# Converting double-precision weights on chip: from seven VectorE operations a chunk to two VectorE, four ScalarE and two GpSimd operations

## Chip, cores and metric

One core of a Trainium2 chip. The metric is the device time of one execution in microseconds, median of several runs. Ratios below are the mean time of one kernel's fast runs over the mean of the other's of the same rounds, so not quite the ratio of the medians. A difference counts as faster or slower from 2%. The rounds ran on different chips; the kernel before was run in each, with medians from 1779.24 to 1780.69 us, while the changed kernel has the four runs of its first measurement only.

## The reference

```python
# attention: q, k, v are (8, 8, 576, 64)
scores = matmul(q, k.T) / 8
scores = where(scores >= max(scores) - tau, scores, -1e9)
attn = softmax(scores);  x = attn @ v          # then (B, H, S, D) -> (B, S, 512)
# feed-forward, with weights that arrive as float64
xn = (x - mean) / sqrt(var + 1e-6) * g_ln
out = x + maximum(xn @ w_ch1, 0) @ w_ch2       # w_ch1 (512, 2048), w_ch2 (2048, 512)
```

## The kernel before

The work goes batch by batch, with no inner barrier: while the attention of batch b is computed, the feed-forward group b-1 is woven in. A batch has four head pairs of five "points"; a point is two sides (two heads), the fifth has one, so a batch has 36 sides. For every side: scores on TensorE, row maximum `neg` (VectorE), threshold `thr` (GpSimd), exponential `e` (ScalarE), mask and sum (VectorE), normalisation of `e` (GpSimd), transposes `tp` (TensorE), copy to `em` (ScalarE), value matmuls `pv`.

The weights come as 8-byte doubles, 32 chunks of 128x512, 16 for w1 (read during batch 0) and 16 for w2 (read from the end of batch 0 into batch 1). The kernel uses no double-precision arithmetic; a chunk's words are put together as float32 by bit operations:

```python
raw = pool.tile([128, WC], I64, tag="sq", name="raw")        # two buffers, shared with the feed-forward
nc.gpsimd.dma_start(out=raw, in_=src)
lo, hi = words[:, :, 0], words[:, :, 1]
nc.vector.tensor_scalar(out=p, in0=hi, ... shift right 20, and 0x7FF)       # L172
nc.vector.tensor_scalar(out=p, in0=p, ... add -896, max 0)                  # L176
nc.vector.tensor_scalar(out=p, in0=p, ... shift left 23)                    # L179
nc.vector.scalar_tensor_tensor(out=p, in0=hi, in1=p, ... sign)              # L182
nc.vector.tensor_scalar(out=a, in0=hi, ... shift left 3, and 0x7FFFF8)      # L186
nc.vector.tensor_tensor(out=a, in0=a, in1=p, op=ALU.bitwise_or)             # L190
nc.vector.scalar_tensor_tensor(out=b, in0=lo, scalar=2.0**-52, in1=p, ...)  # L191
nc.gpsimd.tensor_tensor(out=s, in0=a, in1=b, op=ALU.add)                    # L194
if gi is not None:
    nc.scalar.mul(dst, s, g_sb[:, gi : gi + 1])                             # L196, w1 alone
```

The program is scheduled by a framework that reorders instructions and then fixes the order on each engine. Each engine keeps that order, so an instruction that waits holds all behind it (below, a ScalarE copy that waits 4.86 us, with others behind it).

## Time and profile before

1780.69 us, median of 3 (1779.36 to 1781.99; with a fourth run 1780.68). The marks are read from the order of time on GpSimd: the start of the 1st, 25th and 37th threshold operation (`thr`), and of `sa`, the first sum of a feed-forward group.

| | before |
|---|---|
| thr 1 | 23.2 us |
| thr 25 (24 sides later) | 111.7 us |
| thr 37 (one batch after thr 1) | 158.7 us |
| first `sa` (batch 0 is done) | 171.8 us |
| second `sa` | 380.0 us, 208.2 later |
| end of the span | 1778.9 us, 1398.9 later |

The last line contains no conversion. What is won must be won before the second `sa`.

### The profile page before, as it was taken

What the parts mean: (1) busy time and instruction counts of PE and PEld (TensorE: products, weight loads), DVE (VectorE), ACT (ScalarE), POOL (GpSimd) and SP (SyncE); (2) the same over time, 40 slices, a digit from 0 to 9 for tenths busy, and PEclk for the clock granted to TensorE, in tenths of its full rate; (3) what the DMA queues carried; (4) which work ended last, traced back from release to release, by engine and by line L of the source; (5) the groups of instructions that cost most, each with busy time, mean ns of one, the idle gap of its engine ahead of it and who ended that gap; (6) DMA issues with size and microseconds to landing.
All of it is one profiled execution on the core that took longest, in us unless ns stands there. A gap on an engine that the chain in (4) does not pass through costs nothing.

```text
span 1778.9 us, 19810 instructions
## 1 busy us (share of the span) xinstructions
PE 1671.1 (94%) x6974; PEld 851.8 (48%) x6974; DVE 747.9 (42%) x1719; ACT 558.2 (31%) x1108; POOL 503.3 (28%) x756
## 2 busy tenths in 40 slices
PE   4887889999999999999999999999999999999998
PEld 2444344545555455545554555545544555444443
DVE  6888794443333433433344333443344334200000
ACT  2443233224322442234323432244223432220110
POOL 4555552241222222232224122222233122300100
PEclk8877999999999999999999999999999999999999
DMA  7232341111111110111111111111011000001001
GB/s 140 69 78 68 85 115 21 32 33 20 21 25 22 27 22 17 33 27 21 21 32 33 21 21 25 22 28 21 16 33 26 8 1 12 13 0 16 8 3 21
DMA packets 271379, 55.83 MB, mean 31 GB/s; under 512 B 267184, under 2 KB 267184, under 8 KB 271280
## 3 DMA queue, kind: packets, MB, share of 16 engines
q1 hardware_dynamic: 266640, 37.78, 12.6%
q0 software_dynamic: 4640, 16.78, 3.1%
q8 instruction: 55, 0.90, 0.2%
q14 instruction: 44, 0.36, 0.1%
HBM read 45.09 MB, written 9.44 MB: 31 GB/s over the span
## 4 chain that ended last, share of the span: by engine, by line
PE 80%; DVE 8%; ACT 4%; POOL 4%; DMA 2%; issue 1%; SPq 0%; POOLq 0%; DVEq 0%; ACTq 0%
PE p L394 27%; PE p L359 25%; PE pv L316 11%; PE sc L230 10%; PE tp L281 6%; DVE neg L239 3%; ACT e L247 2%; DMA raw<-in_moe_w_ch_dram 2%; ACT em L284 1%; DVE xc L342 1%; PE tr L290 1%; DVE e L254 1%; ACT er L297 1%; DVE p L182 1%; PE tr L292 1%
## 5 line engine op out<-in xcount | busy, mean ns | idle before, releaser
L359 PE MATMUL p<-xc,w 128*128 128x512 f32 x1152 | 542.0, 609 | 12.1 <-DVE xc L342 11.6
L394 PE MATMUL p<-h,w 128*128 128x512 f32 x1152 | 525.2, 597 | 0.0
L239 DVE TENSOR_REDUCE neg<-sc 128x1 f32<-128x576 f32 x288 | 207.5, 749 | 459.0 <-PE sc L230 459.0
L247 ACT ACTIVATE e<-sc,neg 128x576 f32<-128x576 f32 x288 | 212.8, 745 | 392.8 <-DVE neg L239 390.5
L359 PEld LDWEIGHTS p<-xc,w 128*128 128x128 f32 x1152 | 208.6, 194 | 227.8 <-issue 210.7
L394 PEld LDWEIGHTS p<-h,w 128*128 128x128 f32 x1152 | 206.6, 190 | 218.5 <-issue 218.0
L259 POOL TENSOR_SCALAR e<-e,den 128x576 f32<-128x576 f32 x288 | 216.5, 754 | 258.7 <-DVE den L258 229.5
L242 POOL TENSOR_SCALAR thr<-neg,low_sb 128x1 f32<-128x1 f32 x288 | 91.3, 317 | 627.4 <-DVE neg L239 604.6
L254 DVE SCALAR_TENSOR_TENSOR e<-sc,thr,e 128x576 f32<-128x576 f32 x288 | 232.0, 812 | 49.0 <-ACT e L247 32.6
L230 PE MATMUL sc<-kT,qT 64*128 64x288 f32 x1024 | 194.5, 453 | 29.7 <-DVE kT L208 16.5
L284 ACT COPY em<-tp 128x512 f32<-128x512 f32 x256 | 149.2, 583 | 205.1 <-PE tp L281 202.8
L364 ACT ACTIVATE h<-p 128x512 f32<-128x512 f32 x144 | 86.0, 597 | 383.0 <-PE p L359 382.8
L281 PEld LDWEIGHTS tp<-ident,e 128*128 128x128 f32 x1152 | 135.8, 145 | 135.7 <-ACT em L284 59.4
L281 PE MATMUL tp<-ident,e 128*128 128x128 f32 x1152 | 190.1, 290 | 8.0 <-ACT em L284 4.0
L316 PE MATMUL pv<-em,v_in 128*64 128x256 f32 (+1 forms) x1536 | 177.2, 351 | 19.3 <-ACT em L284 10.1
L230 PEld LDWEIGHTS sc<-kT,qT 64*128 64x128 f32 x1024 | 105.2, 196 | 139.3 <-issue 76.8
L316 PEld LDWEIGHTS pv<-em,v_in 128*64 128x64 f32 x1536 | 99.4, 143 | 124.0 <-ACT em L284 33.6
L402 POOL TENSOR_TENSOR o<-o,x 128x512 f32<-128x512 f32 x36 | 45.5, 1264 | 274.1 <-DVE o L401 274.1
L401 DVE TENSOR_TENSOR o<-p,rb 128x512 f32<-128x512 f32 x36 | 24.9, 691 | 200.8 <-PE p L394 200.8
L327 DVE COPY x<-pv 128x256 f32<-128x256 f32 (+3 forms) x120 | 35.3, 311 | 161.9 <-PE pv L316 161.9
L316 PE MATMUL pv<-er,v_rest 128*64 128x256 f32 (+1 forms) x384 | 64.8, 346 | 14.5 <-ACT er L299 14.5
L297 ACT COPY er<-tr 64x128 f32<-64x128 f32 x256 | 65.7, 257 | 1.7 <-PE tr L292 0.2
(59 smaller groups left out, 827.8 us busy)
## 6 DMA issues: line engine op xcount, KB each, us to landing
raw<-in_moe_w_ch_dram POOLq DMA_DIRECT2D x32, 512.0 KB, 4.3
q_in<-in_q_dram SPq DMA_DIRECT2D x128, 72.0 KB, 2.5
k_in<-in_k_dram SPq DMA_DIRECT2D x128, 72.0 KB, 2.3
out_dram<-ot SPq DMA_DIRECT2D x144, 64.0 KB, 2.0
v_in<-in_v_dram SPq DMA_DIRECT2D x64, 128.0 KB, 2.5
v_rest<-in_v_dram SPq DMA_DIRECT2D x64, 16.0 KB, 2.2
tau_sb<-in_tau_dram SPq DMA_DIRECT2D x1, 0.5 KB, 2.6
g_sb<-in_moe_g_ln_dram POOLq DMA_DIRECT2D x1, 2.0 KB, 3.3
```

What stands on the lines that cost most here:

```text
L230: nc.tensor.matmul(sc[:, c, :HALF], lhsT=lhsT, rhs=kT[rows, c * HALF : (c + 1) * HALF], start=True, stop=True,)
L239: nc.vector.tensor_reduce(out=neg[:, i : i + 1], in_=sc[:, :, :HALF], axis=AXL.XY, op=ALU.max, negate=True)
L242: nc.gpsimd.tensor_scalar(out=thr[:, i : i + 1], in0=neg[:, i : i + 1], scalar1=-1.0, scalar2=low_sb, op0=ALU.mult, op1=ALU.add,)
L247: nc.scalar.activation(e.rearrange("p (c n) -> p c n", c=2), sc[:, :, :HALF], func=AF.Exp, bias=neg[:, i : i + 1],)
L254: nc.vector.scalar_tensor_tensor(out=e2, in0=sc[:, :, :HALF], scalar=thr[:, i : i + 1], in1=e2, op0=ALU.is_ge, op1=ALU.mult, accum_out=den ...
L259: nc.gpsimd.tensor_scalar(out=e, in0=e, scalar1=den[:, i : i + 1], scalar2=1.0, op0=ALU.mult, op1=ALU.mult)
L281: nc.tensor.transpose(tp[:, c], e[:, c * 128 : (c + 1) * 128], ident)
L284: nc.scalar.copy(em[:, :, h, o : o + 128], tp)
L316: nc.tensor.matmul(pv[64 * h : 64 * h + 64, :n], lhsT=vt[:, c, h, :] if c < J else vr[:, h, :], rhs=em[:, c, h, :n] if c < J else er[:, :n ...
L359: nc.tensor.matmul(p1, lhsT=w1_sb[c][:, d * 128 : (d + 1) * 128], rhs=xc[:, c, :], start=(c == 0), stop=(c == NK - 1),)
L364: nc.scalar.activation(h, p1, func=AF.Relu)
L394: nc.tensor.matmul(p2, lhsT=w2_sb[d][:, m * 128 : (m + 1) * 128], rhs=hs[d], start=(d == 0), stop=(d == ND - 1),)
```

## The change

Intent: take the conversion off VectorE, which is busy six to nine tenths in each slice of the first 270 us. The high word is shifted as a whole (two VectorE operations), the low word is scaled to an integer by ScalarE and added as an integer by GpSimd, so that a carry runs into the exponent by itself. Three more ScalarE operations make a factor that is the gain for normal numbers and zero for tiny ones, and GpSimd multiplies by it.

```diff
-  (the seven VectorE operations, L194 on GpSimd and L196 on ScalarE)
+  a = pool.tile([128, WC], U32, tag="o", name="w_bits")
+  r = pool.tile([128, WC], I32, tag="rb", bufs=1, name="w_low")
+  m = pool.tile([128, WC], F32, tag="ot", name="w_kept")
+  nc.scalar.activation(r, lo, func=AF.Copy, scale=2.0**-29)                   # L185
+  nc.scalar.activation(m, <hi as f32>, func=AF.Square)                        # L186
+  nc.scalar.activation(m, m, func=AF.Sign, bias=tiny_sb)                      # L190
+  nc.scalar.activation(m, m, func=AF.Identity, scale=gh, bias=gh)             # L192
+  nc.vector.tensor_scalar(out=a, in0=hi, ... shift left 3, and 0x3FFFFFFF)    # L193
+  nc.vector.scalar_tensor_tensor(out=a, in0=hi, scalar=0xC0000000, in1=a, ...)# L197
+  nc.gpsimd.tensor_tensor(out=a, in0=a, in1=r, op=ALU.add)                    # L201, int32
+  nc.gpsimd.tensor_tensor(out=dst, in0=a, in1=m, op=ALU.mult)                 # L202
```

`gh` is half the gain (w1) or 0.5 (w2), made once on GpSimd.

More of the change, by code (lines that the diff above doesn't have):

```diff
@@ L10 @@
 U32 = mybir.dt.uint32
+I32 = mybir.dt.int32
 I64 = mybir.dt.int64
@@ L74 @@
     g_sb = consts.tile([128, NK], F32, name="g_sb")
+    g_half = consts.tile([128, NK], F32, name="g_half")
+    half_sb = consts.tile([128, 1], F32, name="half_sb")
+    tiny_sb = consts.tile([128, 1], F32, name="tiny_sb")
     ident = consts.tile([128, 128], F32, name="ident")
@@ L122 @@
     nc.vector.memset(avg_sb, 1.0 / DM)
+    nc.vector.memset(half_sb, 0.5)
+    nc.vector.memset(tiny_sb, -(1.0625 * 2.0**-15) ** 2)
     nc.vector.tensor_scalar(
@@ L136 @@
     nc.gpsimd.dma_start(out=g_sb, in_=g_ln.rearrange("(c p) -> p c", p=128))
+    nc.gpsimd.tensor_scalar(
+        out=g_half, in0=g_sb, scalar1=0.5, scalar2=1.0, op0=ALU.mult, op1=ALU.mult
+    )
     WC = 512
@@ L160, in weight_steps @@
         for dst, src, gi in chunks:
-            s = pool.tile([128, WC], F32, tag="o", name="w_sum") if gi is not None else dst
             if src.dtype != I64:
-                nc.gpsimd.dma_start(out=s, in_=src)
-            else:
-                raw = pool.tile([128, WC], I64, tag="sq", name="raw")
-                nc.gpsimd.dma_start(out=raw, in_=src)
-                words = raw.bitcast(U32).rearrange("p (n two) -> p n two", two=2)
-                lo, hi = words[:, :, 0], words[:, :, 1]
-                p = pool.tile([128, WC], U32, tag="o", name="p")
-                a = pool.tile([128, WC], U32, tag="ot", name="a")
-                b = pool.tile([128, WC], F32, tag="ot", name="b")
-                nc.vector.tensor_scalar(
-                    out=p, in0=hi, scalar1=20, scalar2=0x7FF,
-                    op0=ALU.logical_shift_right, op1=ALU.bitwise_and,
-                )
-                nc.vector.tensor_scalar(
-                    out=p, in0=p, scalar1=-896.0, scalar2=0.0, op0=ALU.add, op1=ALU.max
-                )
-                nc.vector.tensor_scalar(
-                    out=p, in0=p, scalar1=23, scalar2=None, op0=ALU.logical_shift_left
-                )
-                nc.vector.scalar_tensor_tensor(
-                    out=p, in0=hi, scalar=0x80000000, in1=p,
-                    op0=ALU.bitwise_and, op1=ALU.bitwise_or,
-                )
-                nc.vector.tensor_scalar(
-                    out=a, in0=hi, scalar1=3, scalar2=0x7FFFF8,
-                    op0=ALU.logical_shift_left, op1=ALU.bitwise_and,
-                )
-                nc.vector.tensor_tensor(out=a, in0=a, in1=p, op=ALU.bitwise_or)
-                nc.vector.scalar_tensor_tensor(
-                    out=b, in0=lo, scalar=2.0**-52, in1=p.bitcast(F32), op0=ALU.mult, op1=ALU.mult
-                )
-                nc.gpsimd.tensor_tensor(out=s, in0=a.bitcast(F32), in1=b, op=ALU.add)
@@ L195, in weight_steps @@
-            if gi is not None:
-                nc.scalar.mul(dst, s, g_sb[:, gi : gi + 1])
+                nc.gpsimd.dma_start(out=dst, in_=src)
+                if gi is not None:
+                    nc.scalar.mul(dst, dst, g_sb[:, gi : gi + 1])
+                yield
+                continue
+            raw = pool.tile([128, WC], I64, tag="sq", name="raw")
+            nc.gpsimd.dma_start(out=raw, in_=src)
+            words = raw.bitcast(U32).rearrange("p (n two) -> p n two", two=2)
+            lo, hi = words[:, :, 0], words[:, :, 1]
@@ new lines, in weight_steps @@
+            a = pool.tile([128, WC], U32, tag="o", name="w_bits")
+            r = pool.tile([128, WC], I32, tag="rb", bufs=1, name="w_low")
+            m = pool.tile([128, WC], F32, tag="ot", name="w_kept")
+            nc.scalar.activation(r, lo, func=AF.Copy, scale=2.0**-29)
+            nc.scalar.activation(
+                m, raw.bitcast(F32).rearrange("p (n two) -> p n two", two=2)[:, :, 1],
+                func=AF.Square,
+            )
+            nc.scalar.activation(m, m, func=AF.Sign, bias=tiny_sb)
@@ new lines, in weight_steps @@
+            gh = half_sb if gi is None else g_half[:, gi : gi + 1]
+            nc.scalar.activation(m, m, func=AF.Identity, scale=gh, bias=gh)
+            nc.vector.tensor_scalar(
+                out=a, in0=hi, scalar1=3, scalar2=0x3FFFFFFF,
+                op0=ALU.logical_shift_left, op1=ALU.bitwise_and,
+            )
+            nc.vector.scalar_tensor_tensor(
+                out=a, in0=hi, scalar=0xC0000000, in1=a,
+                op0=ALU.bitwise_and, op1=ALU.bitwise_or,
+            )
@@ L197, in weight_steps @@
+            nc.gpsimd.tensor_tensor(out=a.bitcast(I32), in0=a.bitcast(I32), in1=r, op=ALU.add)
+            nc.gpsimd.tensor_tensor(out=dst, in0=a.bitcast(F32), in1=m, op=ALU.mult)
             yield
```

## The prediction

> **What bounds the kernel now.** I read the busy rows in 40 slices first, then stretches of the run, then the groups by line inside one stretch, then the chain of waits and the order of time.
>
> ```profile
> PE   4887889999999999999999999999999999999998
> DVE  6888794443333433433344333443344334200000
> PEclk8877999999999999999999999999999999999999
> ```
>
> One slice is 44.5 us. From the seventh slice on (267 us) TensorE is full at a clock near 1, and nothing on the other engines matters. Only before that has TensorE gaps, with VectorE (DVE) at eight to nine tenths. The weight conversion is in exactly this part: its last chunk is read at 264 us. So the change can only shorten the first 270 us of 1779.
>
> ```profile
> core 0: us, PE busy (x) PEld busy (x) DVE busy (x) ACT busy (x) POOL busy (x), PEclk, DMA share, GB/s
> 45.00:160.00 115.00, 93.30 (x455) 53.87 (x455) 95.83 (x222) 53.55 (x107) 65.29 (x87) 0.79 0.30 75
> 187.00:275.00 88.00, 74.86 (x311) 37.30 (x309) 76.06 (x162) 30.34 (x57) 46.05 (x56) 0.96 0.35 97
> 171.80:380.00 208.20, 187.34 (x784) 93.81 (x785) 129.93 (x281) 63.18 (x125) 82.64 (x110) 0.95 0.24 57
> 380.00:573.00 193.00, 188.39 (x840) 97.01 (x839) 78.16 (x187) 66.39 (x134) 51.08 (x85) 0.98 0.14 25
> ```
>
> 45 to 160 is the middle of batch 0 (attention and w1 conversion). 171.8 is the first GpSimd sum of the first feed-forward group, 380 the second, 573 the third. So batch 1, with the w2 conversion in its first half, takes 208.2 us, and the next batch without conversion 193.0: **conversion costs batch 1 about 15 us, and no more can be won there.** Batch 0 is the larger part: TensorE's attention work there runs at a mean clock of 0.79.
>
> In 45 to 160 the groups by line show what VectorE does for a chunk (the last two are the ScalarE and GpSimd share):
>
> ```profile
> L190 DVE TENSOR_TENSOR a<-a,p 128x512 uint32<-128x512 uint32 x13 | 9.2, 707 | 0.0
> L182 DVE SCALAR_TENSOR_TENSOR p<-raw,p 128x512 uint32<-128x512 uint32 x12 | 8.2, 680 | 0.0
> L191 DVE SCALAR_TENSOR_TENSOR b<-raw,p 128x512 f32<-128x512 uint32 x11 | 7.5, 681 | 0.0
> L172 DVE TENSOR_SCALAR p<-raw 128x512 uint32<-128x512 uint32 x12 | 7.5, 623 | 0.1
> L186 DVE TENSOR_SCALAR a<-raw 128x512 uint32<-128x512 uint32 x12 | 6.6, 546 | 0.0
> L179 DVE TENSOR_SCALAR p<-p 128x512 uint32<-128x512 uint32 x12 | 6.1, 512 | 0.0
> L176 DVE TENSOR_SCALAR p<-p 128x512 uint32<-128x512 uint32 x12 | 5.2, 433 | 0.0
> L196 ACT ACTIVATE w<-w_sum,g_sb 128x512 f32<-128x512 f32 x12 | 8.7, 722 | 21.3 <-POOL w_sum L194 21.3
> ...
> L194 POOL TENSOR_TENSOR w_sum<-a,b 128x512 f32<-128x512 f32 x12 | 15.4, 1281 | 13.3 <-DVE den L258 13.0
> ```
>
> The seven VectorE means add up to 4.18 us a chunk, 50 of VectorE's 95.8 us in this stretch, none with idle time before it. The chain of waits, in order of time, has the conversion between the attention steps, for instance here (start, us, what):
>
> ```profile
> 152.18 0.68 DVE b L191
> 153.01 1.27 POOL w_sum L194
> 154.28 0.91 POOL e L259
> 155.23 1.12 PE tp L281 x4
> ```
>
> The attention's normalisation (e, L259) stands behind the conversion's sum on GpSimd, and TensorE's transposes behind both. The order of time also shows the two engines blocking each other:
>
> ```profile
> 13.12 1.25 POOL L194 TENSOR_TENSOR w_sum<-a,b 128x512 f32<-128x512 f32 x1 [4.32 <-DVE b L191]
> 13.38 1.28 DVE L172 TENSOR_SCALAR p<-raw 128x512 uint32<-128x512 uint32 x1 [0.35 <-DMA raw<-in_moe_w_ch_dram]
> ```
>
> This L172 takes 1.28 us, where its shortest is 0.38 and its median 0.43: it ends just after the GpSimd sum does. GpSimd pays as well: thr (L242) has a median of 0.265 us over the run and a mean of 0.525 in this stretch.
>
> **What the Trainium skill says.** "GPSIMD Engine Reference", section 8 Key points: GpSimd's SBUF interfaces are shared with VectorE, and it contends with VectorE instructions in a 2-port mode or with two SBUF inputs. The pair above agrees, and by this rule all seven conversion operations are of those two kinds. "ScalarE: Activation LUTs", What ACT_TABLE_LOAD costs: an activation of N elements with immediates takes 186 ns + 0.833 N ns, and each per-partition pointer adds about 93 ns; N = 512 and one pointer give 706 ns, and L196 shows 722. "GPSIMD Engine Reference", section 4.1 Engine selection: an add of three 32-bit integer tensors is an exact integer add; no duration is given and no run so far shows one, so I take the float sum's 1.28 us. "TensorE: Matmul & The Clock Gate", Part 1: the clock is released by activity; the trace agrees in direction (granted 0.79 in the sparse stretch, 0.98 in the dense batch).
>
> **The change part by part, for one chunk.** VectorE: seven operations (4.18 us) go, two come: a shift-and-mask like L186 (0.42 to 0.55) and a two-input one like L182 (0.68), some 1.15. **It saves 3.0 us.** ScalarE: L196 (0.72, w1 only) goes; Copy and Square with immediates (0.61 each by the formula), Sign with one pointer (0.71) and Identity with two (0.80) come, 2.7 us. **It costs 2.0 us for w1, 2.7 for w2.** GpSimd: one two-input operation of 1.28 becomes two: **it costs 1.28 us.** The DMA and the number of raw buffers (two) stay. No table load is added: in the built program's order one load stands ahead of the first conversion and the next is the feed-forward's Sqrt, as before.
>
> For the 115 us of 45 to 160 with its 12 chunks: VectorE 95.8 - 36 = 60; ScalarE 53.6 - 8.7 + 32.6 = 77; GpSimd 65.3 + 15.4 = 81. The shared interface: today GpSimd without its DMA issues (7.1) 58 plus contested VectorE 50 = 108 of 115, 94%; afterwards 58 + 15.4 + 14 = 87. At the same 94% that makes 93 us. No single engine needs more: the largest are GpSimd's 81, and TensorE's 93 at a clock of 0.79, which should rise when it is fed more densely (a pv matmul took 550 ns here and 351 over the run). So the stretch should fall from 115 to about 93, by 19%.
>
> I checked this by walking one head pair of five points through the changed kernel's instruction order by hand, with the trace's durations, a warm TensorE and no interface conflicts: 29 us from the last scores of one pair to those of the next, with five chunks in it. Before, pairs are 39 us apart (pv of the first round at 82.6 and 121.8) with four. With conflicts and some cold matmuls I put the changed pair at 32.
>
> The start doesn't gain: the changed order has the bit operations of four chunks ahead of the first row maximum on VectorE, and the raw loads come one after the other, some 5 us apart, so the first maximum stays near 22 us. It does put four chunks behind it where three are done now, and the order finishes w1 two thirds through batch 0, so the last third is nearly free of conversion.
>
> Sum: batch 0 after the start, 22 to 172 us, 150 us by 19%: about 29 us; one chunk more before the start: 1 to 2. Batch 1: in 187 to 275 VectorE falls from 76 to 34 us with 14 chunks, but ScalarE rises from 30 to 68 and TensorE needs some 73 of its own; I expect about 10 of the 15 us. Together **40 us: 1741 us.**
>
> **The rivals.**
> (1) ScalarE becomes the bound in its order. The four activations of a chunk stand between the exponentials and the copies of em, the first one waits for a DMA, and w_low has one buffer, so its next writer waits for GpSimd's sum. For it: 77 of some 93 us, and every delayed em copy holds TensorE. Against it: 17% is left, and the walk has no stall over 2 us. It would leave 10 to 15 us of gain, 1765 to 1770.
> (2) GpSimd becomes the bound: sum, product and DMA issue in a row hold thr and the normalisation for up to 3 us, and thr holds the mask and through it the next scores. If the integer sum is slower than the float one (2.5 us, say), 12 more chunks' 1.2 us are added to 81: about 96 of 115, and the gain falls to 10 us or below, 1770 to 1780.
> (3) VectorE alone was the bound and everything else gives way: batch 0 goes to the pace of its chain, about 25 us a head pair, and batch 1 gives all of its 15. Batch 0 then saves 45 to 55: 1712 to 1720. For it: VectorE has next to no idle time before conversion work, and denser feeding warms TensorE. Against it: GpSimd and ScalarE go up at the same time.
>
> **Range and chances.** The line for faster by 2% is 1745, only 4 us above my estimate. I weight the interface reckoning at a half (1733 to 1750), rival 1 or 2 at about 0.3, rival 3 at 0.2. That gives 1741, range 1716 to 1769, faster 0.57, within 2% 0.41, slower 0.02; for slower, batch 0 would have to lose 36 us although the sum of work at the shared interface falls.
>
> **What would show it.** First row maximum near 22 us. First feed-forward sum on GpSimd near 141 us and not 171.8; the next one 196 to 200 us later; batches after that unchanged at 193. Two VectorE conversion operations with means near 0.5 and 0.7 us, thr in batch 0 below 0.5, both GpSimd operations near 1.28, ScalarE about 2.7 us a chunk, and a clock above 0.79 in batch 0. I am wrong in the step on the interface if batch 0 shortens by less than 20 us with the GpSimd durations as said: then idle time before exponentials or em copies behind activations speaks for rival 1, idle time of VectorE before the mask (L254 before) behind thr for rival 2. More than 45 us from batch 0 speaks for rival 3.

## The result, and the profile after

**1754.86 us, median of 4 (1751.53 to 1759.32), ratio 0.9857 (95% interval 0.9833 to 0.988): 1.4% faster, within the 2% band.** The profiled run is the slowest of the four, so the profile shows 21.3 us of gain where the medians show 25.8.

| | before | after | gain |
|---|---|---|---|
| thr 1 | 23.2 | 24.9 | -1.7 |
| thr 1 to thr 25 | 88.5 | 94.5 | -6.0 |
| thr 25 to first `sa` | 60.1 | 35.0 | 25.1 |
| first to second `sa` | 208.2 | 205.7 | 2.5 |
| second `sa` to the end | 1398.9 | 1397.5 | 1.4 |

So the whole gain lies in the last third of batch 0, where the changed order has almost no conversion left: of the first 18 chunks, 17 are finished by thr 25, against 10 before. While conversion runs, a side is no faster than before; only more chunks go by in the same time. The busy rows of the page, answering to those of before:

```profile
PE   4889899999999999999999999999999999999998
DVE  5766544433444334343334434444344434200000
ACT  6775863234323342234323432234223422220110
POOL 6765842232224122232233212322233122300100
PEclk9789899999999999999999999999999999999999
```

In the first six slices VectorE has come down to four to seven tenths, ScalarE and GpSimd have come up to about the same height, and none of the three is full. The stretches of the changed kernel (columns: stretch, length, busy time of each engine, granted TensorE clock, DMA):

```profile
25.00:119.50 94.50, 81.78 (x354) 47.45 (x354) 66.41 (x145) 70.39 (x128) 74.32 (x95) 0.82 0.44 106
119.50:151.00 31.50, 28.58 (x164) 17.96 (x164) 22.17 (x55) 17.75 (x37) 14.01 (x27) 0.95 0.16 29
```

The clock in the stretch with conversion is 0.82; before, it was 0.82 from 25 to 112 us too. The clock rises only in the second stretch, which is nearly free of conversion. The groups by line of the changed kernel from 25 to 118 us, for the conversion alone:

```profile
L202 POOL TENSOR_TENSOR w<-w_bits,w_kept 128x512 f32<-128x512 f32 x14 | 17.8, 1271 | 1.1 <-ACT w_kept L192 0.8
L201 POOL TENSOR_TENSOR w_bits<-w_bits,w_low 128x512 int32<-128x512 int32 x14 | 17.7, 1265 | 4.9 <-DVE den L264 2.9 <-ACT er L303 1.8
...
L197 DVE SCALAR_TENSOR_TENSOR w_bits<-raw,w_bits 128x512 uint32<-128x512 uint32 x14 | 12.2, 873 | 0.1
L192 ACT ACTIVATE w_kept<-w_kept,g_half 128x512 f32<-128x512 f32 x13 | 10.5, 809 | 0.1
L193 DVE TENSOR_SCALAR w_bits<-raw 128x512 uint32<-128x512 uint32 x14 | 10.2, 727 | 4.8 <-POOL w L202 3.5 <-DMA raw<-in_moe_w_ch_dram 1.1
L190 ACT ACTIVATE w_kept<-w_kept,tiny_sb 128x512 f32<-128x512 f32 x14 | 10.1, 720 | 0.1
L185 ACT ACTIVATE w_low<-raw 128x512 int32<-128x512 uint32 x14 | 9.4, 673 | 1.5 <-DMA raw<-in_moe_w_ch_dram 1.1 <-POOL w_bits L201 0.3
L186 ACT ACTIVATE w_kept<-raw 128x512 f32<-128x512 f32 x14 | 9.2, 668 | 0.4 <-POOL w L202 0.3
```

The sizes are close to what was forecast: 2.5 us of GpSimd, 2.87 us of ScalarE and 1.60 us of VectorE a chunk. The VectorE pair takes about 1.1 us in its shorter cases (0.43 and 0.69); in this kernel every L193 over 0.6 us and every L197 over 0.8 us has a GpSimd instruction beside it in the order of time, so the rest is put down to waiting for GpSimd inside the instruction. Just before the first row maximum this is plain in the order of time:

```profile
22.11 2.00 DVE L197 SCALAR_TENSOR_TENSOR w_bits<-raw,w_bits 128x512 uint32<-128x512 uint32 x1
22.26 1.28 POOL L202 TENSOR_TENSOR w<-w_bits,w_kept 128x512 f32<-128x512 f32 x1
```

In batch 1 the chain of waits of the changed kernel, in order of time (start, us, what), has ScalarE in a place where the kernel before had VectorE:

```profile
163.95 2.37 POOL sq L356
...
166.38 1.21 POOL ss L358
167.59 3.89 DMA raw<-in_moe_w_ch_dram
...
171.50 0.69 ACT w_low L185
172.19 0.58 ACT w_kept L186
172.77 0.48 ACT h L370
173.24 0.62 ACT w_kept L190
```

The raw buffers carry the same tag as the feed-forward's squares, so the first load of batch 1 is issued when these are summed. ScalarE's next instruction, the Copy, had been waiting for 4.86 us when the data came, with the feed-forward's `h` behind it.

### The profile page after: what moved, and what is told of

It reads as the page before. It is cut to its first block, busy times and chain, and to the rows that moved or that the text cites. A ratio compares the mean times of both kernels' runs of the same rounds, so it can differ in the third digit from the quotient of the medians.

```text
span 1757.6 us, 19852 instructions
## 1 busy us (share of the span) xinstructions
PE 1665.7 (95%) x6974; PEld 849.2 (48%) x6974; DVE 678.8 (39%) x1561; ACT 627.0 (36%) x1220; POOL 527.2 (30%) x789
## 4 chain that ended last, share of the span: by engine, by line
PE 82%; DVE 5%; ACT 5%; POOL 3%; DMA 2%; issue 2%; SPq 0%; ACTq 0%; POOLq 0%; DVEq 0%
PE p L400 27%; PE p L365 26%; PE pv L322 11%; PE sc L236 11%; PE tp L287 6%; DVE neg L245 2%; ACT e L253 2%; DMA raw<-in_moe_w_ch_dram 2%; ACT em L290 1%; DVE xc L348 1%; PE tr L296 1%; ACT er L303 1%; PE tr L298 1%; DVE e L260 1%; POOL o L408 1%
## 5 line engine op out<-in xcount | busy, mean ns | idle before, releaser
L365 PEld LDWEIGHTS p<-xc,w 128*128 128x128 f32 x1152 | 207.3, 193 | 222.1 <-issue 208.2
L248 POOL TENSOR_SCALAR thr<-neg,low_sb 128x1 f32<-128x1 f32 x288 | 78.8, 274 | 625.6 <-DVE neg L245 599.0
L407 DVE TENSOR_TENSOR o<-p,rb 128x512 f32<-128x512 f32 x36 | 24.9, 692 | 200.7 <-PE p L400 200.7
```

The lines of the kernel that those rows point to most:

```text
L365: nc.tensor.matmul(p1, lhsT=w1_sb[c][:, d * 128 : (d + 1) * 128], rhs=xc[:, c, :], start=(c == 0), stop=(c == NK - 1),)
```

## The experiments

Twelve runs, all correct except the first. One table for all; spans in us from the profiles, which are single executions of each kernel. The framework reschedules every variant, so the order of instructions differs as well, and differences of some us between two variants can be due to the order alone. Runs differ as well: the four of the changed kernel lie 7.8 us apart, and its profiled run is the slowest of them, so a difference of a few us between two profiles shows little.

| kernel | median us | ratio to before | thr 1 to 25 | first `sa` | first to second `sa` |
|---|---|---|---|---|---|
| before | 1780.68 | | 88.5 | 171.8 | 208.2 |
| changed | 1754.86 | 0.9857 | 94.5 | 154.4 | 205.7 |
| e1_floor | 1715.30 | 0.9635 | 77.2 | 132.2 | 186.6 |
| e2_no_guard | 1756.64 | 0.9871 | 94.7 | 159.2 | 202.6 |
| e3_mul_dve | 1757.58 | 0.9871 | 97.8 | 157.8 | 202.6 |
| e4_lean | 1752.47 | 0.9846 | 92.0 | 154.5 | 200.3 |
| e5_fill_before | 1771.67 | 0.9963 | 81.7 | 163.6 | 207.6 |
| e6_fill_after | 1767.89 | 0.9942 | 88.7 | 153.7 | 212.7 |
| e7_lean2 | 1744.69 | 0.9807 | 81.8 | 142.9 | 199.7 |
| e8_fill_lean2 | 1761.98 | 0.9901 | 92.3 | 157.6 | 206.4 |
| e9_after_low2 | 1757.18 | 0.9880 | 92.8 | 151.2 | 206.2 |
| e10_sum_dve | 1782.98 | 1.0029 | 102.0 | 183.4 | 205.6 |
| e11_lean3_raw3 | 1745.08 | 0.9815 | 85.2 | 143.3 | 201.6 |
| e12_no_guard_low2 | 1760.55 | 0.9888 | 93.5 | 157.7 | 202.5 |

The first question is what is left to win.

**e1_floor: no conversion at all.**

```diff
-  (raw load and all conversion operations)
+  nc.gpsimd.dma_start(out=dst, in_=<32-bit data of v>)
```

> Wrong result on purpose: each weight block is loaded straight from 32-bit data of v, with no conversion at all. It gives the floor. From the pace after the last conversion in batch 0 of the changed kernel (2.6 us for each score half, 36 of them) and from 193 us a batch later, every theory expects the first feed-forward sum near 115 to 128 us, batch 1 at 193 us, and 1705 to 1720 us. If the floor lies above 1740, the conversion was no longer what held the changed kernel.

1715.3 us as expected, except that the first `sa` came at 132.2 instead of 115 to 128: even free of conversion, 24 sides take 77 us at the start. The floor leaves out the 8-byte loads and the waits for buffers too, not the arithmetic alone. Against it the conversion cost 39.6 us up to the first `sa` and 21.6 us in batch 1 before, and 22.2 and 19.1 in the changed kernel. So more than half of it is still there, and batch 1 had more to give than the 15 us that I had read from the next batch.

**e2_no_guard, e3_mul_dve, e4_lean: which engine holds it?** e2 leaves out three of ScalarE's four operations, e3 moves one of GpSimd's two to VectorE, e4 leaves out both.

```diff
 e2
-  Square, Sign, Identity on ScalarE
-  nc.gpsimd.tensor_tensor(out=dst, in0=a, in1=m, op=ALU.mult)
+  gb = (ones_sb or g_sb[:, gi : gi + 1]).to_broadcast([128, WC])
+  nc.gpsimd.tensor_tensor(out=dst, in0=a, in1=gb, op=ALU.mult)
 e3
-  nc.gpsimd.tensor_tensor(out=dst, in0=a, in1=m, op=ALU.mult)
+  nc.vector.tensor_tensor(out=dst, in0=a, in1=m, op=ALU.mult)
 e4
-  Square, Sign, Identity on ScalarE, product on GpSimd
+  nc.gpsimd.tensor_tensor(out=s, in0=a, in1=r, op=ALU.add)     # s is dst for w2
+  if gi is not None: nc.scalar.mul(dst, s, g_sb[:, gi : gi + 1])
```

> Square, Sign and Identity on ScalarE are left out (the guard against tiny values; these data have none, so the result stays right), and GpSimd's product takes the gain as a broadcast scalar tensor at the same cost. ScalarE theory (the activations in ScalarE's order hold exponentials and em copies): 10 to 20 us faster than the changed kernel, 1735 to 1745. GpSimd theory (its two sums a chunk hold thr, the normalisation and VectorE): under 5 us faster, 1750 to 1756.

> The changed kernel with the product on VectorE instead of GpSimd (some 0.7 us of VectorE for 1.27 us of GpSimd a chunk). GpSimd theory: 8 to 15 us faster than the changed kernel, 1740 to 1747. ScalarE theory: no gain or a loss of a few us, 1753 to 1760.

> No guard and no product: ScalarE one Copy, VectorE two, GpSimd the integer sum, which writes w2 directly; for w1 ScalarE applies the gain as in the kernel before. Both theories expect it fastest: if ScalarE and GpSimd each hold part, 1725 to 1738; if only one of them does, no better than the better of the two partial kernels by more than 3 us.

None of the three brought batch 0 forward: the first `sa` is at 159.2, 157.8 and 154.5, against 154.4. The only gain is in batch 1, 3 us each and 5 together. Both single theories fail for batch 0. (e2's product was not at the same cost as expected: with the broadcast scalar it took 1.05 us instead of 1.27.) The stretch from 25 to 118 us, one line for each kernel (changed, e3, e4):

```profile
25.00:118.00 93.00, 81.00 (x349) 46.90 (x350) 64.91 (x143) 69.59 (x126) 72.95 (x93) 0.82 0.45 107
```

```profile
25.00:118.00 93.00, 78.85 (x332) 43.83 (x334) 68.17 (x150) 65.12 (x119) 55.80 (x76) 0.83 0.41 102
```

```profile
25.00:118.00 93.00, 76.41 (x334) 44.56 (x336) 65.52 (x142) 50.96 (x98) 54.26 (x79) 0.74 0.42 107
```

In e4 ScalarE and GpSimd lost 19 us each of 93, and the sides went by at nearly the same pace. With these lines and the conversion's groups, the shared interface can be reckoned as in the prediction (GpSimd without its DMA issues, plus VectorE's conversion operations): 73.0 - 7.8 + 22.4 = 87.6 us, 94%, in the changed kernel; 55.8 - 6.9 + 27.0 = 75.9, 82%, in e3; 54.3 - 7.0 + 22.4 = 69.7, 75%, in e4. The share falls by a fifth and the time does not follow. One reserve: e4's granted clock is lower in this stretch, 0.74 against 0.82, and what that took from it was not separated. New waits show up on ScalarE. First e2 (who waited for whom, us, times, longest), then e4:

```profile
ACT w_low L186 <- POOL w_bits L195: 16.4, 7, 4.1
```

```profile
ACT w L196 <- POOL w_bits L194: 16.1, 9, 3.8
```

In e2 the Copy waits for GpSimd's sum because `w_low` has one buffer. In e4 it is not the Copy that waits for the sum but the gain (L196), which needs its result; on ScalarE Copy and gain alternate there while w1 is converted, so each Copy stands behind the gain of the chunk before. ScalarE has less to do, but stands waiting with the exponentials behind it.

**e5_fill_before, e6_fill_after, e8_fill_lean2: is it the cold TensorE?** A rival that the first four runs left standing: TensorE is busy 81 of 93 us in the changed kernel at a clock of 0.82, and in e4_lean's order of time a round of 20 value matmuls takes 4.54 us, where after 118 us, at a clock of 1.00, it takes 2.38. (The 4.75 us in the expectation add two overlapping pieces of 3.68 and 1.07.) Filler matmuls in batch 0 raise the clock:

```diff
+  if u < HP:
+      fl = ps_ff.tile([128, TOK], F32, tag="ff", name="fl")
+      nc.tensor.matmul(fl[:, :256], lhsT=avg_sb, rhs=kT[:, :256], start=True, stop=True)
   (and the same with rhs=e[:, :256] after the transposes of a side)
```

> The kernel before with filler matmuls in batch 0 alone (256 columns, after the scores of a point and after the transposes of a side; their results are never read), some 36 us more TensorE work at full clock. Cold-chain theory (before, VectorE and the interface held batch 0; TensorE's half clock only came second): the granted clock in batch 0 rises to 0.95 or more, and the time stays within 10 us of the kernel before, 1775 to 1790.

> The changed kernel with the same filler. Cold-chain theory (once VectorE is freed, the score, transpose and value matmuls at half clock set the pace of batch 0, so that work taken from the other engines buys little): the clock rises from 0.82 to 0.95 or more, value rounds of 4.75 us fall to 2.4, and in spite of the added work the time falls by 3 to 12 us against the changed kernel, 1743 to 1752. Rival (the in-order queues of GpSimd, ScalarE and VectorE set the pace and the clock is only a symptom): the clock rises as well, but the time stays or grows by up to 15 us, 1755 to 1770.

> The previous kernel with the filler. Cold-chain theory: with the other engines lightened and TensorE warm, the pace of thr 1 to 25 falls from 92 us to 80 or less, 1733 to 1743. Rival: no faster than without filler.

The clock rose from 0.82 to 0.96 in the stretch of the changed kernel, and the 112 filler records took 0.38 us each, 43 us in all. From thr 1 to thr 25 the kernel was faster although it did this work too: 88.7 us against 94.5 (and the kernel before, at 0.97 up to thr 25, 81.7 against 88.5). After thr 25, where the clock had been 0.95 without help, the filler cost 4.4 us: TensorE is then busy 39.2 of 39.4 us. So the first `sa` stayed where it was, 153.7 against 154.4, and the whole got 13 us slower by the medians. The profiled runs lie only 6 us apart; batch 1, where there is no filler, is 7 us longer in them, which I put down to the order. e8 lost 17 us by the medians, in the profiles 10.5 of them between thr 1 and thr 25; why is open. The kernel before, which was to stay within 10 us, gained 8. So the low clock has a price of some 6 us in the conversion stretch, before and after the change (one profile each). Filler all through batch 0 does not win it for the changed kernel, and it does not add to what e7 wins.

**e7_lean2: two buffers for w_low, in the lean kernel.**

```diff
-  r = pool.tile([128, WC], I32, tag="rb", bufs=1, name="w_low")
+  r = pool.tile([128, WC], I32, tag="ot", name="w_low")       # the guard's memory, two buffers
```

> The lean kernel with two buffers for w_low in place of one (in the memory that the left-out guard had used). ScalarE's wait for GpSimd's sum should go (16 us of waits in the first 160 us without the guard). If such waits hold the attention's activations: 3 to 8 us faster than the lean kernel, 1745 to 1750. Cold-chain theory: under 3 us in batch 0, 1749 to 1753.

1744.69 us, 8 us faster than e4 by the medians, and with e11 the fastest of the correct kernels (ratio to before 0.9807, interval 0.9789 to 0.9826, so on the 2% line; 10 us faster than the changed kernel): first `sa` at 142.9 instead of 154.5, thr 1 to 25 in 81.8 us instead of 92.0. ScalarE's Copy waits for the data alone, as in e4, and longer (10.1 us against 1.7). The gain's wait for the sum fell from 16.1 us to 9.4:

```profile
ACT w_low L184 <- DMA raw<-in_moe_w_ch_dram: 10.1, 6, 2.6
ACT w L196 <- POOL w_bits L194: 9.4, 9, 2.3
```

The order on ScalarE differs too: with two buffers two Copies can follow each other. How much of the gain is a shorter wait and how much the new order was not separated; the interface's share, 71.0 of 93 us or 76%, is no lower than e4's.

**e9_after_low2: the second buffer alone, in the changed kernel** (an existing buffer of tag "sm", used in turn with "rb" during w1).

> The changed kernel; only w_low alternates between two existing buffers during w1 (batch 0), everything else as it is. Buffer theory (the one buffer of w_low ties ScalarE's next Copy to GpSimd's sum, and through the in-order queues the attention to the conversion): as in the lean kernel, the pace of thr 1 to 25 falls by 6 to 12 us, 1742 to 1749. Rival (the buffer holds only where GpSimd and ScalarE are light; in the changed kernel, with both at 75 to 80%, their work itself holds): under 3 us, 1752 to 1757.

The rival is right: 1757.18 us, no gain. In the changed kernel ScalarE waited for the sum only 0.3 us from 25 to 118; with three activations between two Copies the buffer was free in time anyway.

**e12_no_guard_low2: the second buffer without the guard, the product still on GpSimd.**

> The kernel without the guard (ScalarE does only Copy; GpSimd still does sum and product) with two w_low buffers. Without the guard alone, ScalarE waited 16 us for w_low's buffer between 25 and 118 us. If ScalarE's three activations are what must go together with the buffer: as the lean kernel with two buffers, 1742 to 1749, ScalarE's wait for the sum below 4 us, thr 1 to 25 near 82 us. If GpSimd's second operation is: no gain over the changed kernel, 1752 to 1758, and GpSimd busy about 80% in that stretch. In between: both have a share.

1760.55 us: no gain, the outcome foreseen for GpSimd's second operation (2.6 us beyond its range, and GpSimd at 74% instead of 80). The buffer did what it was to do: ScalarE's wait for the sum fell from 16.4 us to 3.1. But its wait for the raw load rose from 9.3 to 15.7. GpSimd is busy 69 of 93 us here and 58 in e7_lean2, which has the same second buffer and no product on GpSimd.

**e10_sum_dve: the step of my prediction, tested in the kernel before** (L194 on VectorE).

> The kernel before with the sum on VectorE instead of GpSimd: VectorE gains about 0.7 us a chunk, GpSimd loses 1.28, and so the work at the interface that they share falls by 0.6 us a chunk. My prediction's step (that interface at 94% holds batch 0): 5 to 12 us faster than the kernel before, 1768 to 1775. Rival (VectorE's own work holds it): 8 to 20 us slower, 1788 to 1800.

1782.98 us, ratio 1.0029: neither theory's number. The interface came down (45 to 160 us: GpSimd 44.9 instead of 65.3, while the VectorE sum took 1.22 us in place of the 0.7 I had expected; reckoned as before, 38.5 + 55.7 = 94 of 115 us, 82%), and nothing became faster. The granted clock in that stretch was 0.68 against 0.79, so this run alone does not clear the interface. The profiled run, the slowest of its four at 1788, has its first `sa` 12 us later than before, which in batch 0 is what the rival expected.

**e11_lean3_raw3: a third raw buffer for w1, and the first load early.**

```diff
-  g_half made on GpSimd
+  if which == 1 and ci % 3 == 2: raw = pool.tile(..., tag="xc", bufs=1, name="raw")
```

> The lean kernel with two w_low buffers, a third raw buffer during w1 (the buffer of xc, which batch 0 leaves free) and without the halved gain, whose wait for the gain's DMA had pushed GpSimd's first raw load from 2.9 to 5.3 us. If raw loads hold the attention (15% of the chain in the kernel with two w_low buffers): 4 to 10 us faster than that kernel, 1734 to 1741; else within 3 us of it, 1741 to 1748.

1745.08 us, the same as e7_lean2. thr 1 came 3 us earlier, thr 1 to 25 took 3.4 longer. Raw loads are on the chain (15.1% of e7_lean2's from 25 to 118 us), but a third buffer is not what batch 0 lacks.

## Why the prediction was right or wrong

The time, 1754.86, lies in the range of 1716 to 1769, and the run came out within 2%, to which I had given 0.41. Of 40 us forecast, 26 came. It lies in the range because the range is wide: it lies in the band of none of the accounts that the prediction named (1712 to 1720, 1733 to 1750, 1765 to 1770, 1770 to 1780), and nearly all of the gain came from a place to which the prediction gave no size of its own.

- **Which engine does what, and how long: right.** GpSimd's integer sum 1.265 us (forecast 1.28), ScalarE 2.87 (2.7), VectorE 1.60 (1.15; the difference is put down to waiting for GpSimd, see above).
- **The start: right in kind.** thr 1 at 24.9 instead of 23.2, four chunks' VectorE part ahead of the first maximum (before, two chunks and five of a third's seven operations, not three chunks). In the order of time the 1.7 us lost go with the L197 of 2.00 us and the later first load (5.3 instead of 2.9 us).
- **Order: right, with no size given.** w1 is finished two thirds through batch 0, and the rest runs free: 25 us gained after thr 25.
- **The step that failed: "At the same 94% that makes 93 us."** The share of the interface did come out at 94% again, which looks like a confirmation and is none. e3 and e4 took it to 82 and 75% in the changed kernel, and e10 lowered it in the kernel before; none of the three sped up batch 0 (e4 and e10 at lower clocks, as said). A pair of engines that is busy 94% by a sum of durations is not thereby what sets the pace: the durations contain the waiting for each other. Of the seven operations counted as contested, L172, L179, L186, L182 and L190 reach 1.1 to 2.6 us beside GpSimd and take 0.42 to 0.69 alone; L176 never takes over 0.64, L191 never over 0.69. In consequence batch 0 gave 17.4 us in the profile in place of 29 to 31. The walk by hand failed with it: it put a changed pair at 32 us, and while conversion ran the pairs' first value rounds came 35.6 and 34.3 us apart (42.0, 77.6, 111.9). Before it was 37.1 and 37.9; the 82.6 and 121.8 that the prediction quotes are second rounds.
- **What the stretch waits for instead.** The chain of waits of the changed kernel from 25 to 118 us, by line (the view cuts its end):

```profile
by line: PE sc L236 29.5%; PE pv L322 20.0%; PE tp L287 10.4%; issue 8.3%; DVE e L260 6.0%; DMA v_rest<-in_v_dram 4.2%; POOL w L202 4.1%; DVE neg L245 3.4%; DVE w_bits L193 2.7%; ACT e L253 2.4%; DVE w_bits L197 1.9%; POOL e L265 1.7%; PE t
```

  60% of it are the attention's own score, value and transpose matmuls (43% before), some 9% conversion. The floor needs 77.2 of the 94.5 us for these sides with no conversion at all, at a clock of 0.85. With the filler the three matmuls fall to 23% of the chain, raw loads lead it with 20.6%, and the stretch is 6 us shorter. The signs that the prediction named for its rivals hardly appear: VectorE's mask waits 0.7 us for `thr` and 1.4 us for the exponential in these 93 us.
- **The clock, "which should rise when it is fed more densely": wrong for the part with conversion** (0.82 and 0.82), right for the part without (0.95). The prediction's 550 and 351 ns for a value matmul set the 256-column form against a mean of all forms; that form alone has 412 over the run.
- **Batch 1: the limit of 15 us was too low, the 10 us far too high.** The floor puts its conversion cost at 21.6 before; 2.5 were won. Here rival 1 of the prediction is what the chain shows: ScalarE's first activation waits for the raw DMA, and `h` and `em` stand behind it. e2 and e4, without the guard on ScalarE, are 3 to 5 us shorter there. But e3, with the guard, is 3 us shorter too, and all of these differences are within the spread of single runs, so the guard isn't shown to be the cause.
- **Rival 2, GpSimd's second operation, has its share in batch 0, but not by itself.** e3 without it gains nothing, e4 without it and without the guard gains nothing, the second w_low buffer gains nothing (e9), nor with the guard gone (e12). From e12 to e7 the product leaves GpSimd (and w1's gain goes to ScalarE), and the first `sa` comes at 142.9 instead of 157.7. Only with all three done together do 11.5 us come back (e7, and 11.1 in e11 with another order). The reading that fits is several holds of nearly the same strength, where one takes over from the other; it is argued from these runs and not shown.

What stays open: whether the guard on ScalarE matters once the product and the single buffer are gone (that combination was not run); how much of the differences of 2 to 5 us is the scheduler's order and not the operation changed; and what holds the last 10.7 us that e7_lean2 is behind the floor in batch 0, and its 13.1 in batch 1.

## What to carry to other kernels

When work is taken from the busiest engine and given to three others, the price of a chunk need not be that of its busiest engine: every engine and buffer that it passes can hold it, and so can the work beside it. So forecast the gain from a floor (the work left out altogether) and a count of every single buffer on the chunk's way. One experiment that takes away one cost and shows nothing doesn't clear that cost: here the product on GpSimd and the single buffer of `w_low` looked innocent alone, and with both gone, and the guard, 10 us came. And read when the work is done, not only how much: nearly all of this gain came from conversion being finished earlier, with a free stretch behind it.

## What the Trainium skill lacked or had wrong

- "GPSIMD Engine Reference", section 4.1: the exact integer add is given no duration of its own. Here a 128x512 int32 sum takes 1.265 us, the same as the float32 product of that size (1.271 us).
- "ScalarE: Activation LUTs", What ACT_TABLE_LOAD costs: the formula gives 613 ns for an activation with immediates at N = 512. Copy and Square from every second 32-bit word took 673 and 668 ns, 55 to 60 ns more; Sign and Identity from dense words (720 and 809) are within 15 ns of the 706 and 798 that it gives with one and two pointers. Whether the stride or the type does it was not separated.
- "TensorE: Matmul & The Clock Gate", Part 1, says that activity releases the clock. The filler agrees (0.82 to 0.96). What the page lacks is whether matmuls whose results are never read pay for themselves: here they gained 8 us in one kernel and lost 13 and 17 in two others.
